# One load of a streaming decode kernel split by rows into sixteen loads of 1 to 15 rows

## The chip, the core and the metric

The kernel runs on one core of one Trainium2 chip. Times are device microseconds of one execution. The time before is 704.22 us, the median of three runs (703.95 to 704.27). The profile comes from one further execution, which took 704.12 us.

## The reference

A decode step of four sequences passes twice through the same pair of layers: grouped-query attention over a cache of 4096 positions, then a gated feed-forward block. Both passes use the same weights and the same caches, all in f32.

```python
B, Sq, D = 4, 1, 512
Hq, Hkv, Sk, Dh = 32, 8, 4096, 128          # F = 1792
q = (x @ wq).reshape(B, Sq, Hq, Dh)         # each K/V head serves 4 query heads
scores = einsum("bhqd,bhkd->bhqk", q, k) * Dh ** -0.5
o = einsum("bhqk,bhkd->bhqd", softmax(scores), v)
A = o.reshape(B, Sq, Hq * Dh) @ wo
h = silu(x @ w1) * (x @ w3);  B_ = h @ w2
x = x + A(layernorm(x)); x = x + B_(layernorm(x))     # and both once more
```

## The kernel before

**The data.** The host lays weights and caches side by side in one array `in_rows` of 128 rows. One unit of it is `KB` = 256 floats, so 1 KB of each row, 128 KB in all. Weights, and then the K and V tiles of each K/V head `g`, stand in the order of `stream`; a K or V tile is 4 units wide, `("kv", g, r)` with `r` from 0 to 31, the first 16 of K and the rest of V.

**The loads.** All data pass through one on-chip buffer, `space`, of 218 units (`SPACE`). The table `LOADS` lists every load by hand, in order: `(source unit, number of units, place in space)`. The function `pump` walks through the table and issues a load (L140; the first is on L137) as soon as its whole place is free; a place is set free by `done`, which the program calls after the last matmul that reads a tile. All loads are issued by SP, in the table's order, and go to one DMA queue. So a load that has to wait on SP holds up every later one.

**Completion counters.** The framework gives each load the next of eight completion counters in turn (`DMAHW0_49` to `DMAHW7_49` in the rows below). Before a load may take its counter, SP waits until the load eight places earlier, which had the same counter, has landed. Waits on `PE_49` mean that the place still has to be read by matmuls.

**The work.** Layer 0 goes through the heads 0 to 7, layer 1 from 7 back to 0, so that part of what is on the chip serves twice. For each head, `score` multiplies the query by the K tiles (L322), `maximum` and `exponent` make the softmax of half a head, `turn` transposes it and `weigh` multiplies it by the V tiles (L387). The weights follow: `project_o`, `gather_o`, `share_q`, and `feed_forward` with `down` (L503).

**The place of the change.** In layer 1, head 3, the entries `(544, 36, 148)` and `(580, 28, 190)` bring the V tiles `r` = 16 to 24 and 25 to 31. The last tile, `("kv", 3, 31)`, has its source at unit 604 and its place at 214. After it stand `(320, 64, 28)` and `(8, 24, 92)`, loads for the next heads, and `(384, 64, 154)`, whose place covers that of the last tile.

Of the kernel before, what the change touches and what calls it, by code (L numbers as in the profile page):

```python
# [16 lines left out]
P = 128  # L17
# [25 lines left out]
KB = 256  # L43
# [16 lines left out]
    (868, 8, 68), (876, 4, 186), (880, 4, 190), (884, 8, 194), ("stash", 1, 202), (892, 8, 206), ("stash", 0, 214),  # L60
# [5 lines left out]
)  # L66
BUSY = (4, 1, 2)
SCRATCH = 64

# [5 lines left out]
def tile_decode_layers(ctx: ExitStack, tc: tile.TileContext, rows, out):  # L75
    nc = tc.nc
# [9 lines left out]
    def place(at, n):  # L86
        return space[:, at * KB:(at + n) * KB]
# [32 lines left out]
    def pump():  # L120
        while state["next"] < len(LOADS):
            src, n, at = LOADS[state["next"]]
            if src == "stash":
                i, n = n, U // KB
                keys = [("kv", TURN, i)]
                if i == 0 and not state["back"]:
                    return
            else:
                keys = [key for key in stream if src <= offset[key] < src + n]
            if any(taken[at:at + n]):  # L130
                return
            taken[at:at + n] = [True] * n
            if src == "stash":
                for j in range(2):
                    nc.scalar.activation(place(at, n)[:, j * BLOCK:(j + 1) * BLOCK], stored[2 * i + j], AF.Copy)
            elif state["next"] == 0:
                nc.sync.dma_start(space[:, at * KB:], rows[:, 0:n * KB + P])  # L137
            else:
                lo = src * KB + (P if src >= LOADS[0][1] else 0)
                nc.sync.dma_start(place(at, n), rows[:, lo:lo + n * KB])  # L140
            for key in keys:
                where[key] = at
                at += size[key[0]]
            state["next"] += 1
# [4 lines left out]
    def done(layer, *key):  # L149
        if layer == 0 and (key[0][:2] == "w1" or key[0] in ("wq", "wo") and key[1] >= HELD or key[:2] == ("kv", TURN) and key[2] in KEPT):  # L150
            return
        at, n = where[key], size[key[0]]
        taken[at:at + n] = [False] * n
        pump()

    pump()


# [40 lines left out]
    def busy(n):  # L199
        if n:  # L200
            pt = scores().rearrange("p (k c) -> p k c", k=KC)
            nc.tensor.matmul(pt[:, 0:n, :], ident, ident.unsqueeze(1).to_broadcast([P, n, P]),  # L202
                             start=True, stop=True)
# [31 lines left out]
    def layernorm():  # L235
        xc, sq = deviation()
        xT = lay_down(xc)
        squares(xc, sq)

        def factor():  # L240
            var = o_ps[1][:, 1:2]
            mean(var, ssq)
            inverse(rstd[:, 0:1], var)

        return xT, factor
# [173 lines left out]
    def turn_o(o, oT):  # L419
        nc.tensor.matmul(misc[:, 0:B * REP], o, head, start=True, stop=True)  # L420
        nc.vector.tensor_copy(oT[:, :, 0:B], misc[:, 0:B * REP].rearrange("p (b h) -> p h b", b=B))  # L421
# [5 lines left out]
    def project_o(layer, g, oT):  # L427
        w = wo_of(g)
        for h in range(REP):
            for k in range(KC):  # L430
                nc.tensor.matmul(x_ps[32 * k:32 * k + B, :], oT[:, h, 0:B], w[:, h, k * P:(k + 1) * P],  # L431
                                 start=(h == 0), stop=(h == REP - 1))
        done(layer, "wo", g)
        nc.vector.scalar_tensor_tensor(x_sb, x_ps, 1.0, x_sb, op0=ALU.mult, op1=ALU.add,
                                       accum_out=rowsum)
# [107 lines left out]
    for layer in range(LAYERS):  # L543
# [13 lines left out]
        for n, (g, (first, last)) in enumerate(order):  # L557
# [7 lines left out]
            if layer and n == 0:  # L565
                state["back"] = True
                pump()
# [22 lines left out]
        nc.scalar.activation(spare, half[:, 0:1], AF.Sigmoid)  # L590
        busy(BUSY[0])
        turn_o(o, oT)
        busy(BUSY[1])
        project_o(layer, g, oT)
        busy(BUSY[2])
        xT, factor = layernorm()
# [50 lines left out]
```

## Time and profile before

| | |
|---|---|
| median of three runs | 704.22 us (703.95 to 704.27) |
| the profiled execution | 704.12 us, span 702.3 us |
| PE busy | 421.3 us (60%), 3280 matmuls |
| VectorE, ScalarE busy | 144.5 us (21%), 41.7 us (6%) |
| SP's DMA queue | 12960 packets, 297.41 MB, 99.0% of sixteen engines' time |
| rate over the span | 424 GB/s |
| mean granted TensorE clock | 0.825 |

The span is the time between the first and the last instruction of the profile; 1.8 us of the execution lie around it. PE is the matrix engine, SP the engine that issues the loads. "DMA share" in a table of stretches is the mean busy share of the core's sixteen DMA engines. "SPq" marks an instruction of SP's sequencer; in the timeline such rows are merged, "x4" with the time from the first start to the last end. In rows on DMA issues, the last number is the time from issue to landing, for the loads issued in the stretch that was asked for. Sizes are of all 128 rows together.

### The profile page before, as it was taken

How to read it: one execution, taken by the hardware profiler on the slowest of the kernel's cores; microseconds unless marked ns; L12 is line 12 of the kernel's file. 1: busy time of each engine (PE TensorE's matmuls, PEld its weight loads, DVE VectorE, ACT ScalarE, POOL GpSimd, SP SyncE). 2: the span in 40 equal slices, each digit the busy share in tenths (PEclk: the TensorE clock that was granted, in tenths of full speed). 3: DMA queues.
4: the chain of work that ended last, by engine and by line, in shares of the span. 5: the costliest groups of instructions: out<-in, count | busy, mean ns of one | idle time of the engine just before them, and what ended most of it. 6: DMA issues, size and time to landing. Idle time of an engine off the chain costs nothing.

```text
span 702.3 us, 7502 instructions
## 1 busy us (share of the span) xinstructions
PE 421.3 (60%) x3280; PEld 133.4 (19%) x3280; DVE 144.5 (21%) x512; ACT 41.7 (6%) x100; POOL 3.1 (0%) x10
## 2 busy tenths in 40 slices
PE   1265466644578409667688985744555734567576
PEld 0111121201112103121124221201111211121223
DVE  2012112121023103330231322112120301213221
ACT  0010000100001001000101210000100001000100
POOL 0000000000000000000000000000000000000000
PEclk9997677876769859886999997877877958779999
DMA  9999999999999999999999999999999999999996
GB/s 422 418 415 425 467 419 418 426 457 417 449 414 444 424 438 415 436 423 427 422 418 378 423 430 440 439 438 418 441 440 414 450 419 448 430 425 417 424 425 268
DMA packets 12991, 297.87 MB, mean 424 GB/s; under 512 B 1440, under 2 KB 1568, under 8 KB 4512
## 3 DMA queue, kind: packets, MB, share of 16 engines
q1 hardware_dynamic: 12960, 297.41, 99.0%
q8 instruction: 25, 0.41, 0.2%
q14 instruction: 6, 0.05, 0.0%
HBM read 297.34 MB, written 0.07 MB: 423 GB/s over the span
## 4 chain that ended last, share of the span: by engine, by line
DMA 71%; PE 24%; DVE 1%; another core or an unknown queue 1%; ACT 1%; issue 1%; SPq 0%; ACTq 0%; DVEq 0%
DMA space<-in_rows 71%; PE o L387 10%; PE scores L322 9%; PE sums_ps L306 1%; PE turned L348 1%; ACT p L341 1%; PE scores L202 1%; PE stored L251 1%; DVE acc L335 0%; DVE pT L350 0%; PE o L463 0%; SPq L140 0%; PE sums_ps L431 0%; PE sums_ps L420 0%
## 5 line engine op out<-in xcount | busy, mean ns | idle before, releaser
L322 PE MATMUL scores<-space,qT 128*32 128x512 f32 x1024 | 170.0, 713 | 141.6 <-DMA space<-in_rows 140.8
L387 PE MATMUL o<-space,pT 128*16 128x512 f32 x1024 | 152.8, 710 | 99.3 <-DMA space<-in_rows 91.5
L322 PEld LDWEIGHTS scores<-space,qT 128*32 128x32 f32 x1024 | 36.0, 123 | 218.6 <-issue 180.0
L387 PEld LDWEIGHTS o<-space,pT 128*16 128x16 f32 x1024 | 31.7, 108 | 198.3 <-issue 94.2
L335 DVE TENSOR_REDUCE acc<-scores 128x1 f32<-128x512 f32 x32 | 22.1, 691 | 181.5 <-PE scores L322 181.5
L341 ACT ACTIVATE p<-scores,acc 128x512 f32<-128x512 f32 x30 | 20.6, 687 | 559.0 <-DVE acc L335 432.1
L410 DVE SCALAR_TENSOR_TENSOR o<-o,acc,o 128x128 f32<-128x128 f32 x112 | 39.3, 351 | 49.2 <-PE o L387 45.8
L350 DVE COPY pT<-turned 128x256 f32<-128x256 f32 x32 | 13.6, 425 | 154.3 <-PE turned L348 154.3
L348 PE MATMUL turned<-ident,p 128*128 128x128 f32 x128 | 21.9, 296 | 11.8 <-ACT p L341 11.8
L295 PE MATMUL sums_ps<-space,xT 128*32 128x512 f32 x120 | 22.9, 704 | 2.4 <-DMA space<-in_rows 2.4
L421 DVE COPY o<-sums_ps 128x16 f32<-128x16 f32 x16 | 2.8, 175 | 98.1 <-PE sums_ps L420 98.1
L348 PEld LDWEIGHTS turned<-ident,p 128*128 128x128 f32 x128 | 14.0, 145 | 44.1 <-ACT p L341 25.7
L306 PEld LDWEIGHTS sums_ps<-same,shares 128*128 128x128 f32 x120 | 16.3, 211 | 16.8 <-DVE shares L301 11.1
L306 PE MATMUL sums_ps<-same,shares 128*128 128x4 f32 x120 | 17.6, 270 | 0.9 <-DVE shares L301 0.9
L463 PE MATMUL o<-space,xT 128*32 128x192 f32 (+1 forms) x256 | 13.7, 355 | 3.2 <-DMA space<-in_rows 1.5
L441 PE MATMUL stored<-space,o 128*32 128x512 f32 x104 | 13.5, 592 | 0.0
L301 DVE TENSOR_SCALAR shares<-sums_ps,columns 128x512 f32<-128x512 f32 x15 | 11.1, 743 | 1.7 <-PE sums_ps L295 1.7
L503 PE MATMUL sums_ps<-space,hT 128*4 128x128 f32 x224 | 9.1, 272 | 3.6 <-DMA space<-in_rows 2.9
L211 PE MATMUL o<-columns,same 128*32 128x1 f32 x64 | 2.0, 181 | 14.3 <-DVE columns L548 13.3
L420 PEld LDWEIGHTS sums_ps<-columns,o 128*128 128x128 f32 x32 | 6.1, 239 | 20.6 <-issue 13.0
L463 PEld LDWEIGHTS o<-space,xT 128*32 128x32 f32 x256 | 7.6, 110 | 8.4 <-DVE h L480 2.8
L420 PE MATMUL sums_ps<-columns,o 128*128 128x16 f32 x32 | 7.7, 318 | 0.6 <-DVE o L410 0.6
(101 smaller groups left out, 141.9 us busy)
## 6 DMA issues: line engine op xcount, KB each, us to landing
space<-in_rows SPq DMA_DIRECT2D x11, 4096.0 KB, 21.6
space<-in_rows SPq DMA_DIRECT2D x14, 1024.0 KB, 18.6
space<-in_rows SPq DMA_DIRECT2D x3, 4608.0 KB, 24.6
space<-in_rows SPq DMA_DIRECT2D x2, 6144.0 KB, 30.9
space<-in_rows SPq DMA_DIRECT2D x6, 2048.0 KB, 29.2
space<-in_rows SPq DMA_DIRECT2D x3, 3584.0 KB, 23.5
space<-in_rows SPq DMA_DIRECT2D x2, 5120.0 KB, 28.7
space<-in_rows SPq DMA_DIRECT2D x1, 7680.0 KB, 33.8
```

The lines of the kernel that those rows point to most:

```text
L295: nc.tensor.matmul(wide[32 * k:32 * k + 32, :], xT[:, 32 * k:32 * k + 32], w[:, k, :], start=True, stop=True)
L306: nc.tensor.matmul(misc[:, h * B:(h + 1) * B], shares[:, h * DH:(h + 1) * DH], same[:, 0:B], start=True, stop=True)
L322: nc.tensor.matmul(ps[32 * b:32 * b + 32, :], qT[:, b, at:at + 32], t[:, i * BLOCK:(i + 1) * BLOCK], start=(m < 2), stop=(m >= TILES - 2))
L335: nc.vector.tensor_reduce(acc[:, i:i + 1], ps, axis=AX.X, op=ALU.max, negate=True)
L341: nc.scalar.activation(p.rearrange("p n s -> p (n s)"), ps, AF.Exp, bias=acc[:, i:i + 1], scale=1.0 if scale is None else scale, accum_out ...
L348: nc.tensor.transpose(pt[:, n, :], p[:, n, :], ident)
L350: nc.vector.tensor_copy(pT, pt.rearrange("p n (b r) -> p n b r", b=B)[:, :, :, 0:ROW])
L387: nc.tensor.matmul(o_ps[i][32 * b:32 * b + ROW, :], pT[:, r // 2, b, :], t[:, j * NB * DH:(j + 1) * NB * DH], start=(r < 2), stop=(r >= TI ...
L410: nc.vector.scalar_tensor_tensor(o, o_ps[s][:, j * DH:(j + 1) * DH], acc[:, 16 + NB * s + j:17 + NB * s + j], o, op0=ALU.mult, op1=ALU.add)
L420: nc.tensor.matmul(misc[:, 0:B * REP], o, head, start=True, stop=True)
L441: nc.tensor.matmul(bank[32 * h:32 * h + 32, :], oT[:, h, :], w[:, h, :], start=first, stop=last)
L463: nc.tensor.matmul(bank[32 * j:32 * j + 32, s], xT[:, 32 * k:32 * k + 32], w[:, j], start=(k == 0), stop=(k == KC - 1))
```

## The change

The entry `(580, 28, 190)` is cut in two: `(580, 24, 190)` and `(604, 4, 214)`. The second, 4 KB of each of the 128 rows, is issued as sixteen DMAs: of 1 row, of 2, 3 and so on to 15, and of the 8 rows that remain. Sources and places in `space` stay as they were, and every other load too.

```diff
-    (580, 28, 190), (320, 64, 28), (8, 24, 92), (384, 64, 154), (192, 64, 28), (256, 64, 140), (32, 32, 28),
+    (580, 24, 190), (604, 4, 214), (320, 64, 28), (8, 24, 92), (384, 64, 154), (192, 64, 28), (256, 64, 140), (32, 32, 28),
...
+BY_ROWS = 604
+ROWS = 0, 1, 3, 6, 10, 15, 21, 28, 36, 45, 55, 66, 78, 91, 105, 120, P
...
-                nc.sync.dma_start(place(at, n), rows[:, lo:lo + n * KB])
+                for a, b in zip(ROWS, ROWS[1:]) if src == BY_ROWS else ((0, P),):
+                    nc.sync.dma_start(place(at, n)[a:b], rows[a:b, lo:lo + n * KB])
```

On SP, before, around the place of the change; the sizes are rows x floats of each row, so 128x9216 is the entry `(544, 36, 148)`, 128x7168 the entry `(580, 28, 190)`, and 128x16384 and 128x6144 behind it are `(320, 64, 28)` and `(8, 24, 92)`:

```order
L140 DMA space<-in_rows 128x9216 [waits DMAHW3_49,DMAHW1_49,PE_49]
L140 DMA space<-in_rows 128x7168 [waits PE_49]
L140 DMA space<-in_rows 128x16384 [waits DMAHW2_49,PE_49]
L140 DMA space<-in_rows 128x6144 [waits PE_49]
L140 DMA space<-in_rows 128x16384 [waits DMAHW4_49,DMAHW3_49,PE_49]
```

On SP in the changed kernel, the first rows of the same place; 128x6144 is now `(580, 24, 190)`:

```order
L143 DMA space<-in_rows 128x9216 [waits DMAHW3_49,DMAHW1_49,PE_49]
L143 DMA space<-in_rows 128x6144 [waits PE_49]
L143 DMA space<-in_rows 1x1024 [waits PE_49]
L143 DMA space<-in_rows 2x1024
L143 DMA space<-in_rows 3x1024
L143 DMA space<-in_rows 4x1024 [waits DMAHW0_49]
L143 DMA space<-in_rows 5x1024
L143 DMA space<-in_rows 6x1024 [waits DMAHW2_49]
```

The rows that follow them:

```order
L143 DMA space<-in_rows 7x1024 [waits DMAHW3_49]
L143 DMA space<-in_rows 8x1024 [waits DMAHW4_49]
L143 DMA space<-in_rows 9x1024 [waits DMAHW5_49]
L143 DMA space<-in_rows 10x1024 [waits DMAHW6_49]
L143 DMA space<-in_rows 11x1024 [waits DMAHW7_49]
L143 DMA space<-in_rows 12x1024 [waits DMAHW0_49]
L143 DMA space<-in_rows 13x1024 [waits DMAHW1_49]
L143 DMA space<-in_rows 14x1024 [waits DMAHW2_49]
L143 DMA space<-in_rows 15x1024 [waits DMAHW3_49]
L143 DMA space<-in_rows 8x1024 [waits DMAHW4_49]
L143 DMA space<-in_rows 128x16384 [waits DMAHW5_49,PE_49]
L143 DMA space<-in_rows 128x6144 [waits DMAHW6_49,PE_49]
```

Sixteen issues stand between the load of 3072 KB and that of 8192 KB. The load of 3072 KB has counter 4, the sixteen have the counters 5, 6, 7, 0 and so on round twice, and the load of 8192 KB has counter 5 again. The seventh small load waits on counter 3 for the load of 9216 floats a row; the eighth waits on counter 4 for the 3072 KB load; the ninth to the sixteenth wait for the first to the eighth; the load of 8192 KB waits on counter 5 for the ninth.

On PE, in `weigh` of head 3, the last rows that read the split tile, before and now:

```order
L387 MATMUL o_95<-space,pT 16x512 [waits DVE_49]
L387 MATMUL o_95<-space,pT 16x512
L387 MATMUL o_95<-space,pT 16x512 [waits DMAHW4_49]
L387 MATMUL o_95<-space,pT 16x512 x13
L322 MATMUL scores<-space,qT 32x512 [waits DMAHW5_49,PE_49]
```

```order
L390 MATMUL o_95<-space,pT 16x512 [waits DVE_49]
L390 MATMUL o_95<-space,pT 16x512
L390 MATMUL o_95<-space,pT 16x512 [waits DMAHW4_49]
L390 MATMUL o_95<-space,pT 16x512 x11
L390 MATMUL o_95<-space,pT 16x512 [waits DMAHW4_49,DMAHW5_49,DMAHW3_49,DMAHW6_49,DMAHW2_49,DMAHW7_49,DMAHW1_49,DMAHW0_49]
L390 MATMUL o_95<-space,pT 16x512
L325 MATMUL scores<-space,qT 32x512 [waits DMAHW5_49,PE_49]
```

The last two matmuls of the half head now wait for all eight counters, that is for the sixteen small loads; before, all tiles from `r` = 25 on came with one wait.

## The prediction

> **What bounds the kernel now.** I read the page first: its head, the slices, the queue and the chain that ended last.
>
> ```profile
> span 702.3 us, 7502 instructions
> DMA  9999999999999999999999999999999999999996
> q1 hardware_dynamic: 12960, 297.41, 99.0%
> DMA 71%; PE 24%; DVE 1%; another core or an unknown queue 1%; ACT 1%; issue 1%; SPq 0%; ACTq 0%; DVEq 0%
> ```
>
> The sixteen DMA engines are busy in every slice but the last, SP's queue alone fills 99.0% of their time, and the chain is 71% DMA. So the kernel lasts as long as 297 MB take to stream in, and what counts is any moment at which a DMA engine has nothing queued. Next I asked for busy time and DMA share in stretches around the changed load, from there to the end, and at the end.
>
> ```profile
> core 0: us, PE busy (x) PEld busy (x) DVE busy (x) ACT busy (x) POOL busy (x), PEclk, DMA share, GB/s
> 545.00:550.00 5.00, 5.00 (x44) 1.97 (x42) 0.55 (x2) 0.00 (x0) 0.00 (x0) 1.00 1.00 430
> 558.00:694.00 136.00, 80.96 (x685) 26.95 (x685) 28.38 (x100) 7.68 (x18) 0.55 (x1) 0.81 1.00 427
> 694.00:695.00 1.00, 0.63 (x17) 0.32 (x16) 0.41 (x3) 0.00 (x0) 0.00 (x0) 1.00 0.92 348
> 695.00:696.00 1.00, 0.73 (x28) 0.72 (x32) 0.00 (x0) 0.00 (x0) 0.00 (x0) 1.00 0.62 234
> 696.00:697.00 1.00, 0.72 (x29) 0.39 (x20) 0.00 (x0) 0.00 (x0) 0.00 (x0) 1.00 0.48 184
> 697.00:698.00 1.00, 0.45 (x20) 0.22 (x13) 0.00 (x0) 0.00 (x0) 0.00 (x0) 1.00 0.23 86
> 698.00:699.00 1.00, 0.80 (x24) 0.24 (x12) 0.00 (x0) 0.00 (x0) 0.00 (x0) 1.00 0.06 23
> ```
>
> The share is 1.00 up to 694 us, so a stall of the queue around 550 us finds no idle time later that could take it up. At the end the share falls in steps: the engines run out one by one over some 4.5 us, so they are uneven, and the slowest sets the end. The idle shares of those five rows add up to 2.7 us; that is the most that perfectly even engines could save.
>
> **The place of the change.** SP's issues and the DMA issues of narrow windows give the load that is split (3584 KB), the one behind it (third row of the second fence, where its 8192 KB stand without a size), and the load of 4608 KB before it.
>
> ```profile
> 520.83 0.33 SPq L140 DMA_DIRECT2D space<-in_rows  x1
> 525.56 32.82 SPq L140 DMA_DIRECT2D space<-in_rows  x4
> 545.36 4.84 SPq L140 DMA_DIRECT2D space<-in_rows  x2
> ```
>
> ```profile
> space<-in_rows SPq DMA_DIRECT2D x1, 4608.0 KB, 24.6
> space<-in_rows SPq DMA_DIRECT2D x1, 3584.0 KB, 28.3
> space<-in_rows SPq DMA_DIRECT2D x1, 27.9
> ```
>
> The load of 3584 KB is issued at 525.56 and lands 28.3 later, at 553.9. The next, of 64 rows of KB, is issued at 545.36 and lands at 573.3: its 8192 KB take 573.3 - 553.9 = 19.4 us, or 422 KB per us, 26.4 for each engine. When it is issued, 8.5 us of queue are still ahead of it. That is the cover which the change must not use up.
>
> **The change part by part.** Removed: 512 KB of the one load, 512/422 = 1.2 us of streaming. Its first 3072 KB keep their place and now land at about 552.7. The same 512 KB come back as sixteen loads, so the bytes cost nothing by themselves.
>
> Added: the sixteen issues, and their waits. The order shows that each load takes the next of eight completion counters, and that SP waits before a load until the load eight places earlier has landed. The seventh small load waits for the load of 4608 KB, so until 520.83 + 24.6 = 545.4; the eighth waits for the 3072 KB load itself, so until 552.7. Behind it on SP stand eight more small loads and then the load of 8192 KB, which before went out at 545.36. So the queue runs dry: at 552.7 the engines have only the 28 rows of seven small loads left. That is the term that decides, and it has two unknowns: the price of an issue, and that of starting the engines again.
>
> Issue:
>
> ```profile
> L140 SPq DMA_DIRECT2D space<-in_rows x88: 327/328/1182, 1.2 to 686.2; - x88
> 652.17 1.75 SPq L140 DMA_DIRECT2D space<-in_rows  x4
> ```
>
> Four issues in a row take 1.75 us, 0.44 each; the instruction alone has a median of 0.328 us. No issue of fewer than 128 rows is in the trace. The lower bound is 0.33; the upper is 0.44 with one slow one (1.18) among the nine. I take 0.44. The wait ends at 552.7 plus some 0.05, the eighth to sixteenth small loads are nine issues, and the big load is the tenth: 552.75 + 9 x 0.44 = 556.7. The small loads' own waits do not hold this up: the sixteenth waits for the eighth, issued 3.5 us before.
>
> Starting again:
>
> ```profile
> 0.74 0.38 SPq L137 DMA_DIRECT2D space<-in_rows  x1
> space<-in_rows SPq DMA_DIRECT2D x1, 4160.0 KB, 12.2
> out<-space SPq DMA_DIRECT2D x1, 64.0 KB, 1.5
> ```
>
> The program's first load meets idle engines: 4160 KB in 12.2 us, of which 4160/422 = 9.9 are streaming, so 2.3 us lie between issue and landing beyond the stream. The store at the end also meets idle engines: 1.5 - 64/422 = 1.35 us. The bounds are 1.35 and 2.3; I take 2.3, since that row is a load of the same kind on all sixteen engines. The Trainium skill, page "DMA: Bandwidth & Descriptors", section "Anatomy of one DMA", puts the fixed part of a DMA at about 2.0 us (measured on another issuing path); by that figure the sum below would be 0.3 us less, and the trace's 2.3 agrees roughly.
>
> Sum: the big load's stream now ends 2.3 + 19.4 us after 556.7, at 578.4; before it landed at 573.3. That is 5.1 us later, and each load behind it is as much later, since the share of 1.00 leaves no room. The 1.2 us of bytes are in the sum already: they land while SP issues.
>
> Priced at nothing: PE's matmuls on the split tile. They are the last of these:
>
> ```profile
> 554.37 3.67 PE o L387 x32
> 558.06 41.85 DMA space<-in_rows
> ```
>
> The sixteenth small load is issued at 552.75 + 8 x 0.44 = 556.3 and lands at 557.8 to 558.6, while PE now finishes the tile at 558.04. So PE, and with it the load that SP issues at 558.06 when that space is free, may be up to 1 us later. That load has 11,264 KB queued ahead of it (8192, and the 3072 of the second issue in the row of 545.36), 26.7 us, which hide it.
>
> The 16 engines start afresh together after the gap. The lead that the faster ones had at 550 us is lost, and that costs nothing, since the slowest sets each landing.
>
> Base and result: the profiled execution took 704.12 us with a span of 702.3 and 1.8 around it; the median of the runs is 704.22, 0.1 more. 704.12 + 5.1 = **709.2 us**.
>
> **The rivals.**
>
> *The queue does not run dry.* If SP could send the sixteen loads well before 550 us, only the uneven shares would act. If a load of n rows uses n engines with one row each, the first engine gets sixteen rows of 4 KB instead of eight and the last none: 8 x 4/26.4 = 1.2 us more and 1.2 us less. With the late engine of the end rows among those relieved, the time would be 704.12 - 1.2 = 702.9; with it among the loaded ones, 705.3. It decides if the eighth small load goes out more than a microsecond or two before the 3072 KB have landed. Against it stands the wait in the order; for it, that the engines are uneven indeed. The Trainium skill, same page, section "Why a DMA increments its semaphore by 16 and not by 1", says that a DMA on this queue takes the largest number of engines up to 16 that divides its slowest dimension, and the lowest-numbered ones; no row here shows it.
>
> *The stall is made up later.* Then the time stays at 704.1. It needs 5 us of idle DMA after 558 us; the row of 558 to 694 has 1.00, which speaks against it.
>
> *The small loads land late.* If the eighth takes not 1.5 but the shortest time that a load shows here, 5.1 us, the sixteenth waits for it until 552.75 + 5.1 = 557.85, and the big load goes out at 558.3: 6.7 us, 710.8. The row:
>
> ```profile
> DMA to landing us min/median/max: 5.1/21.0/51.5
> ```
>
> Against it: those loads had others queued ahead, these do not.
>
> *Each small load pays its way alone.* If the eighth to sixteenth followed each other at 1.5 us, issue to landing, the big load would go out at 552.75 + 9 x 1.5 = 566.3, 9.6 us later than forecast: 718.8. Against it: four issues stand within 1.75 us, long before any of them lands, and the counters make a load wait for the eighth before it only. The Trainium skill, same page, section "Rules for kernel authors", says that transfers under 64 KB pay mostly overhead and are to be joined into larger ones; that speaks against this change, and as far as the stall of 5.1 us goes I expect the trace to agree.
>
> **How the numbers follow.** Chances: the stall as summed 0.80; late landing 0.08; one by one 0.03; no dry queue 0.05 (0.03 faster, 0.02 slower); made up later 0.04. About 0.2%, 1.4 us, is what a measurement of this kernel can tell from no change. So slower 0.93, same 0.04, faster 0.03. The range takes in both unknowns: low ends, 9 x 0.33 and 1.35, give 552.75 + 3.0 + 1.35 - 553.9 = 3.2, or 707.3; the high ends, 0.44 with one issue of 1.18 (4.7 us) and 2.3, give 5.9, or 710.0. I stretch it to the late landing, 710.9. One by one, no dry queue and made up later, 0.12 together, stay outside.
>
> **What the new profile would show.** DMA share well under 1.00 between about 552 and 558 us, where it is 1.00 now; the sixteen issues, of which the last nine come in one run after 552.7 and about 0.44 apart; the 8192 KB load issued near 556.7 instead of 545.36; later pieces of the chain late by about 5 us. I am wrong if the 8192 KB load still goes out before 552 us, if the share stays at 1.00, or if the late pieces win back what the gap cost. If the gap is there with another length, the price of an issue or of the restart is the step that failed.

## The result, and the profile after

The changed kernel takes 709.18 us (median, 708.84 to 710.56) against 704.25 in runs beside it: ratio 1.0069, 95% interval 1.0055 to 1.0082, so slower. The prediction was 709.2. The profiled execution took 709.12 us with a span of 707.3, 5.0 more than before on both counts.

The page of the changed kernel, its head, queue and chain:

```profile
span 707.3 us, 7525 instructions
DMA  9999999999999999999999999999999899999997
q1 hardware_dynamic: 13216, 297.41, 98.5%
DMA 73%; PE 23%; DVE 1%; another core or an unknown queue 1%; SPq 1%; issue 1%; ACT 0%; DVEq 0%; ACTq 0%
```

The same 297.41 MB now fill 98.5% of the engines' time instead of 99.0%, the slice that holds the place of the change (548 to 566 us) has an 8, and SP's sequencer is now 1% of the chain instead of 0%. SP's timeline gives the run of small loads and the 8192 KB load behind them; the chain shows the same place step by step.

```profile
526.29 1.94 SPq L143 DMA_DIRECT2D space<-in_rows  x6
534.39 11.18 SPq L143 DMA_DIRECT2D space<-in_rows  x2
552.74 3.31 SPq L143 DMA_DIRECT2D space<-in_rows  x9
556.15 0.36 SPq L143 DMA_DIRECT2D space<-in_rows  x1
```

```profile
526.29 26.43 DMA space<-in_rows
552.72 0.02 issue
552.74 0.27 SPq L143
553.01 0.04 issue
553.05 0.29 SPq L143
...
555.32 0.38 SPq L143
555.71 0.04 issue
555.75 1.93 DMA space<-in_rows
```

The 3072 KB load and five small ones go out from 526.29 on; the sixth waits until 534.39, the seventh until 545.3, the eighth until the 3072 KB have landed at 552.72. Then nine small loads are issued in a row, and the load of 8192 KB goes out at 556.15, 10.8 us later than before. The stretches show what the DMA engines did meanwhile:

```profile
core 0: us, PE busy (x) PEld busy (x) DVE busy (x) ACT busy (x) POOL busy (x), PEclk, DMA share, GB/s
545.00:550.00 5.00, 5.00 (x46) 2.09 (x48) 0.92 (x4) 0.17 (x1) 0.00 (x0) 1.00 0.98 419
551.00:553.00 2.00, 2.00 (x16) 0.61 (x8) 0.00 (x0) 0.00 (x0) 0.00 (x0) 1.00 0.13 49
553.00:555.00 2.00, 1.48 (x17) 0.48 (x20) 1.73 (x11) 0.00 (x0) 0.00 (x0) 1.00 0.29 78
555.00:557.00 2.00, 2.00 (x19) 0.32 (x8) 1.32 (x5) 0.00 (x0) 0.00 (x0) 1.00 0.53 127
558.00:694.00 136.00, 76.82 (x620) 24.54 (x624) 26.68 (x96) 7.41 (x18) 0.55 (x1) 0.80 0.99 424
```

For six microseconds the queue moves 49 to 127 GB/s instead of over 400. Afterwards it is full again. (These views count a packet whole in the stretch in which it starts, so shares and rates of short stretches are rough, and a share can pass 1.00. With each packet of the trace spread over its own time, the three stretches from 551 to 557 us have shares of 0.25, 0.27 and 0.54.)

### The profile page after: what moved, and what is told of

It reads as the page before. It is cut to its first block, busy times and chain, and to the rows that moved or that the text cites. A ratio compares the mean times of both kernels' runs of the same rounds, so it can differ in the third digit from the quotient of the medians.

```text
span 707.3 us, 7525 instructions
## 1 busy us (share of the span) xinstructions
PE 420.5 (59%) x3280; PEld 135.5 (19%) x3280; DVE 144.4 (20%) x512; ACT 41.7 (6%) x100; POOL 3.0 (0%) x10
## 3 DMA queue, kind: packets, MB, share of 16 engines
q1 hardware_dynamic: 13216, 297.41, 98.5%
## 4 chain that ended last, share of the span: by engine, by line
DMA 73%; PE 23%; DVE 1%; another core or an unknown queue 1%; SPq 1%; issue 1%; ACT 0%; DVEq 0%; ACTq 0%
DMA space<-in_rows 73%; PE o L390 10%; PE scores L325 7%; PE turned L351 1%; PE sums_ps L309 1%; SPq L143 1%; PE stored L254 1%; PE sums_ps L298 0%; DVE pT L353 0%; DVE o L413 0%; PE o L466 0%; PE sums_ps L434 0%; PE scores L205 0%; ACT p L344 0%
## 5 line engine op out<-in xcount | busy, mean ns | idle before, releaser
L325 PE MATMUL scores<-space,qT 128*32 128x512 f32 x1024 | 173.3, 724 | 154.6 <-DMA space<-in_rows 153.9
L390 PE MATMUL o<-space,pT 128*16 128x512 f32 x1024 | 145.8, 675 | 90.1 <-DMA space<-in_rows 81.9
L351 PE MATMUL turned<-ident,p 128*128 128x128 f32 x128 | 23.5, 312 | 10.4 <-ACT p L344 10.4
L298 PE MATMUL sums_ps<-space,xT 128*32 128x512 f32 x120 | 24.4, 736 | 4.3 <-DMA space<-in_rows 4.3
L309 PEld LDWEIGHTS sums_ps<-same,shares 128*128 128x128 f32 x120 | 17.8, 227 | 17.4 <-DVE shares L304 10.2
L309 PE MATMUL sums_ps<-same,shares 128*128 128x4 f32 x120 | 19.1, 282 | 0.9 <-DVE shares L304 0.9
```

What stands on the lines that cost most here:

```text
L298: nc.tensor.matmul(wide[32 * k:32 * k + 32, :], xT[:, 32 * k:32 * k + 32], w[:, k, :], start=True, stop=True)
L309: nc.tensor.matmul(misc[:, h * B:(h + 1) * B], shares[:, h * DH:(h + 1) * DH], same[:, 0:B], start=True, stop=True)
L325: nc.tensor.matmul(ps[32 * b:32 * b + 32, :], qT[:, b, at:at + 32], t[:, i * BLOCK:(i + 1) * BLOCK], start=(m < 2), stop=(m >= TILES - 2))
L351: nc.tensor.transpose(pt[:, n, :], p[:, n, :], ident)
L390: nc.tensor.matmul(o_ps[i][32 * b:32 * b + ROW, :], pT[:, r // 2, b, :], t[:, j * NB * DH:(j + 1) * NB * DH], start=(r < 2), stop=(r >= TI ...
```

## The experiments

Two theories stood against each other first. *Dry queue*: the eighth small load waits for the load before the sixteen, so the queue runs empty; the price depends on how many loads follow it. *The small loads themselves*: each costs a fixed amount, or they burden the engines unevenly. The runs change the number and the form of the small loads; where a run also cuts the load before them, this is said.

### Six loads, seven, sixteen and thirty-two with even shares

```diff
-ROWS = 0, 1, 3, 6, 10, 15, 21, 28, 36, 45, 55, 66, 78, 91, 105, 120, P
+ROWS = 0, 16, 32, 48, 64, 96, 128
...
+ROWS = 0, 16, 32, 48, 64, 80, 96, 128
...
+ROWS = 0, 16, 32, 48, 64, 80, 96, 112, 128
+PARTS = 2
...
+                    w = n * KB // PARTS if src == BY_ROWS else n * KB
+                    for c in range(0, n * KB, w):
+                        nc.sync.dma_start(place(at, n)[a:b, c:c + w], rows[a:b, lo + c:lo + c + w])
```

The first line is that of six loads, the second that of seven; the rest is that of sixteen, and thirty-two differ from it by `PARTS = 4`.

> The same 512 KB as six loads (four of 16 rows, two of 32), all on sixteen engines. Theory (the queue runs dry, because a small load that stands eight places behind the 3072 KB load has to wait for its landing): the 8192 KB load now stands seven places behind, so it waits only for the load of 4608 KB and goes out near 545.4 as before; DMA share stays 1.00 around 550 us; 704.2 us. Rival 'each small load costs a fixed amount' (5.0 us / 16 = 0.31 each): 704.2 + 6 x 0.31 = 706.1. Rival 'uneven shares of the engines': shares are even here, 704.2.

> The same 512 KB as seven loads (six of 16 rows, one of 32). Theory (dry queue): now the 8192 KB load itself stands eight places behind the 3072 KB load, so it goes out at 552.8 instead of 545.4; no issue stands between, but the engines have at most the small loads, 1.2 us, to cover a restart of 2.3 to 2.7 us; 704.2 + 1.1 to 1.5 = 705.3 to 705.7. Rival 'fixed amount each': 704.2 + 7 x 0.31 = 706.4, only 0.3 above the six loads. Rival 'uneven shares': 704.2.

> The same 512 KB as sixteen loads of 16 rows x 2 KB each, so all on sixteen engines, 32 KB each. Theory (dry queue): as in the changed kernel, nine issues and a restart after the landing at 552.7; issues of 16 rows are taken at 0.43 instead of the 0.38 measured there: 5.0 + 9 x 0.05 = 5.4 later, 709.6. Rival 'fixed amount each': 709.2. Rival 'uneven shares': shares are even, 704.2.

> The same 512 KB as thirty-two loads of 16 rows x 1 KB. Theory (dry queue): twenty-five issues of 0.43 and a restart after 552.7: the 8192 KB load goes out at 552.75 + 25 x 0.43 = 563.5, 7.4 later than in the changed kernel, so 709.2 + 7.4 = 716.6. Rival 'fixed amount each': 704.2 + 32 x 0.31 = 714.2. Rival 'uneven shares': 704.2.

Measured, beside 703.97 of the kernel before: six 706.7 (ratio 1.0037, 1.0025 to 1.0049), seven 706.79 (1.0049, 1.0037 to 1.0062), sixteen 710.2 (1.0088, 1.0075 to 1.0101), thirty-two 717.58 (1.0193, 1.018 to 1.0206). Even shares do not save anything, so the uneven shares are not the cause. Sixteen and thirty-two follow the dry queue (709.6 and 716.6) within 1.0 us; sixteen would fit the fixed price as well (709.2), thirty-two would not (714.2). But six was expected at 704.2 and took 2.7 more, and fits the fixed price (706.1) better. Seven, expected at 705.3 to 705.7, took 1.1 more than that, and only 0.1 more than six: in this form the step from six to seven does not show in the time. The stretches of six:

```profile
545.00:550.00 5.00, 5.00 (x50) 2.20 (x52) 1.11 (x5) 0.40 (x1) 0.00 (x0) 1.00 1.01 415
550.00:553.00 3.00, 2.79 (x24) 0.76 (x14) 0.53 (x3) 0.68 (x3) 0.00 (x0) 1.00 1.29 314
553.00:557.00 4.00, 3.21 (x26) 0.72 (x30) 2.90 (x14) 0.00 (x0) 0.00 (x0) 1.00 1.06 342
```

There is no gap: the DMA share is over 1.00 while the rate is only 314 and 342 GB/s. The engines were busy but slow. (With each packet spread over its own time, the shares are 1.03 and 1.01, the rates 255 and 284 GB/s.) In the trace's packet records the 4 KB packets took 0.273 us (median), and the last packets of the 3072 KB load, which ran beside them, 1.58 us where 0.91 is usual. So a second cost exists, and the next runs take it apart.

### Six loads in two other forms, and seven

The same 512 KB as six loads of all 128 rows with 512 or 768 B of each; as six loads of 32 rows that lie four rows apart; and as seven loads of all rows.

```diff
+PIECES = [(slice(0, P), slice(a, b)) for a, b in ((0, 128), (128, 256), (256, 448), (448, 640), (640, 832), (832, 1024))]
...
+PIECES = [(slice(r, P, 4), slice(a, b)) for r, a, b in ((0, 0, 1024), (1, 0, 1024), (2, 0, 512), (2, 512, 1024), (3, 0, 512), (3, 512, 1024))]
...
+                for rs, cs in PIECES if src == BY_ROWS else ((slice(0, P), slice(0, n * KB)),):
+                    nc.sync.dma_start(place(at, n)[rs, cs], rows[:, lo:lo + n * KB][rs, cs])
```

> After the six loads of 16 to 32 neighbouring rows, which cost 2.7 us with no gap in the queue: their packets of 4 KB took about 0.28 us beside each other, 1.8 times the 0.156 of a lone one, so the new theory is that many engines writing to few neighbouring rows get in each other's way. Here the 512 KB go as six loads of all 128 rows, 512 or 768 B of each. Theory (dry queue from the seventh load on, and neighbouring rows slow): neither applies, 704.2 us, the 8192 KB load issued near 545.4. Rival 'each extra small load costs by itself' (2.7 / 6 = 0.45 each): 706.7.

> Six loads again, of 32 rows each, four rows apart (4 KB of each row in two of them, 2 KB in four). Theory (neighbouring rows get in each other's way): the same number of rows in a load as in the larger of the six loads before, but spread over all 128, so no loss: 704.2. Rival 'few rows or small loads are slow wherever they lie': 706.7, as with neighbouring rows.

> Seven loads of all 128 rows, 512 or 768 B of each. Theory (dry queue): one load more than six puts the 8192 KB load eight places behind the 3072 KB load; it goes out at 552.8 instead of 545.4, and the restart is only partly covered: 705.3 to 705.7, that is 1.1 to 1.5 above the six loads of all rows. Rival 'each extra small load costs by itself': 704.2 + 7 x 0.45 = 707.4 if the six loads of all rows take 706.7, and no step between six and seven.

Measured, beside 704.01: all rows 704.38 (ratio 0.9999, 0.9985 to 1.0014), four rows apart 704.09 (0.9995, 0.9979 to 1.001), seven 705.53 (1.0013, 0.9999 to 1.0027). Six loads more cost nothing if they cover all rows or their rows are spread, so a fixed price for each load falls. Rates of the six loads of all rows, then of those four rows apart (384 and 426, then 420 and 432 GB/s, with each packet spread over its own time):

```profile
550.00:553.00 3.00, 3.00 (x28) 0.65 (x20) 1.23 (x6) 1.08 (x3) 0.00 (x0) 1.00 1.28 476
553.00:557.00 4.00, 3.48 (x34) 1.25 (x36) 2.92 (x14) 0.00 (x0) 0.00 (x0) 1.00 1.05 450
```

```profile
550.00:553.00 3.00, 3.00 (x27) 0.89 (x20) 0.81 (x6) 1.07 (x3) 0.00 (x0) 1.00 1.20 498
553.00:557.00 4.00, 3.48 (x35) 0.92 (x33) 3.06 (x14) 0.00 (x0) 0.00 (x0) 1.00 1.12 484
```

And the step from six to seven loads is there in SP's timeline, six first: the first issue of each row is the 8192 KB load.

```profile
545.25 0.33 SPq L143 DMA_DIRECT2D space<-in_rows  x1
```

```profile
552.71 0.81 SPq L143 DMA_DIRECT2D space<-in_rows  x2
```

One small load more moves it from 545.25 to 552.71, as the counters have it. The time rises by 1.15 us in the medians, in the expected range (705.3 to 705.7); by the ratio alone, seven loads are only just not distinguished from before.

### Sixteen spread loads in one go, and woven

Sixteen loads of 32 rows x 1 KB, four rows apart: once in one go, once in fours between three pieces of 1024 KB; and the changed kernel's own sixteen loads woven in the same way.

```diff
+LAST = [(slice(r, P, 4), slice(24 * KB + c, 25 * KB + c)) for r in range(4) for c in range(0, 4 * KB, KB)]
+PIECES = [q for i in range(4) for q in (*LAST[4 * i:4 * i + 4],
+          *[(slice(0, P), slice(8 * i * KB, 8 * i * KB + 8 * KB))][:i < 3])]
```

> Sixteen loads of 32 rows x 1 KB, the rows four apart (which cost nothing in the six strided loads), in one go as in the changed kernel. Theory (dry queue): issues of such loads stood 0.62 apart in the run of six, so nine of them take 5.6 us instead of 3.4: 709.2 + 2.2 = 711.4. Rival 'neighbouring rows make the loss of the changed kernel': no neighbours here, 704.2.

> The very same sixteen strided loads, but woven in fours between the 3072 KB, which go as three loads of 1024 KB: four small, one large, four small, one large, and so on. No load waits for one that stands last in the queue, and something is always left in it. Theory (dry queue): 704.2 to 705.5, with the 8192 KB load issued before the last of the large pieces has landed. Rival 'sixteen more loads cost what they cost wherever they stand': 711.4, as in one go.

> The changed kernel's own sixteen loads of 1 to 15 neighbouring rows, woven in the same way. Theory: without the dry queue only the price of neighbouring rows is left, which was 2.7 us for six loads of 16 and 32 rows: 705 to 707.5. Rival 'the sixteen row loads cost 5.0 us wherever they stand': 709.2.

Measured, beside 704.23: in one go 711.35 (ratio 1.0101, 1.0087 to 1.0115), woven 706.58 (1.0033, 1.0022 to 1.0045), own rows woven 706.65 (1.0044, 1.003 to 1.0058). SP's run of nine small loads and the 8192 KB load, in one go, and its stretch:

```profile
552.84 6.19 SPq L143 DMA_DIRECT2D space<-in_rows  x10
```

```profile
553.00:557.00 4.00, 3.48 (x29) 0.81 (x28) 3.06 (x14) 0.00 (x0) 0.00 (x0) 1.00 0.17 41
```

Without neighbouring rows the sum of the dry queue comes out at once: 711.4 expected, 711.35 measured. The very same loads, woven, are 4.8 us faster. That they are not at 704.2 to 705.5, as expected, is mostly because the weave was too loose: the share is 0.76 from 545 to 550 us, so the queue ran partly dry there. At the 430 GB/s of the kernel before, the bytes of that stretch would have taken 2.1 us less, of the 2.4 that this run lost. The 8192 KB load went out at 552.88, 2 us before the last of the large pieces landed (554.84), as expected, but long after 545.4.

```profile
545.00:550.00 5.00, 5.00 (x44) 1.97 (x42) 0.55 (x1) 0.00 (x0) 0.00 (x0) 1.00 0.76 252
```

The changed kernel's own loads, woven, cost 2.4 us instead of 4.9. How much of these 2.4 is the loose weave and how much neighbouring rows was not separated.

### Uneven shares without a dry queue: two attempts

```diff
+PIECES = [(slice(32, P), slice(0, 12 * KB)), *((slice(r, 32, 4), slice(0, 12 * KB)) for r in range(4))]
...
+ROWS = 0, 127, 128
```

> Uneven shares without a dry queue: the load of 28 rows of KB is cut into 16 and 12, and the 12 KB part goes as one load of 96 rows and four of 8 rows that lie four rows apart. If a load of 8 rows uses the first eight engines only, they get ten rows of 12 KB each and the others six instead of eight: 24 KB or 0.9 us more and less. The 8192 KB load stands six places behind the 2048 KB load, so no gap. If the late engines of the end are in the second half: 703.3; if they are in the first half: 705.1; if a load of 8 rows is spread over all sixteen: 704.2.

> Uneven shares alone: the 512 KB as two loads, of 127 rows and of 1 row, 4 KB each; only three places from the 3072 KB load to the 8192 KB load, so no dry queue. The Trainium skill, page 'DMA: Bandwidth & Descriptors', section 'Why a DMA increments its semaphore by 16 and not by 1', names 127 partitions as a case that uses one engine. By rows of this case: one engine then carries 127 packets of 0.156 us, 19.8 us instead of 1.2, and ends 18.6 us later less the lead it has over the slowest, 0 to 4.5 us: 718.3 to 722.8. If the 127 rows are spread over the engines, or the other engines take over, 704.2. The distance tells what an uneven share costs when no other cause hides it.

The first took 708.53 (ratio 1.0055, 1.0038 to 1.0072) where 703.3 to 705.1 was expected. It says nothing on shares: while its pieces ran, the rate fell with the engines busy, as with the six loads of neighbouring rows. The slow stretch begins with the load of 96 neighbouring rows, ahead of those of 8: in the packet records its 12 KB packets take 0.9 us from 548 us on, where 0.46 is usual, and the 16 KB packets of the load before them 1.2 instead of 0.61. So loads of few rows are not the only slow ones.

```profile
549.00:553.00 4.00, 4.00 (x34) 1.06 (x27) 1.48 (x6) 1.07 (x3) 0.00 (x0) 1.00 1.07 232
```

The second took 728.63 (1.0356, 1.0339 to 1.0373), 6 us over its range of 718.3 to 722.8. One engine did carry the 127 rows: the share between 550 and 555 us is 0.15, and the trace has 4 KB packets one behind the other from 549.5 to 578 us. Its 8192 KB load had landed on fifteen engines by 581.87 us and on the sixteenth at 598.73, 25.5 us later than before (573.26); the whole time is 24.7 us longer. The expectation lacked two things. The 127 packets took 28.8 us rather than 19.8: 0.16 each until 557.7 us, but 0.28 on average once 64 KB packets of the other engines ran beside them. And SP was held up, as its timeline has it:

```profile
525.33 30.68 SPq L143 DMA_DIRECT2D space<-in_rows  x2
```

```profile
550.00:555.00 5.00, 4.48 (x40) 1.28 (x36) 2.25 (x14) 1.08 (x3) 0.00 (x0) 1.00 0.15 61
```

The issue of the single row behind the 127 did not end until 556.0, so the 8192 KB load was late too, and the other engines stood idle. So this run shows that a large uneven share is paid by the one engine that has it, but the price of a small one stays open. That the changed kernel's loss is not that of uneven shares follows from the sixteen spread loads, and from its own packet records: the first sixteen packets of the 8192 KB load, read here as one for each engine, begin between 557.14 and 557.92 us, so by then no engine had a backlog left.

## Why the prediction was right

**The dry queue** was the step that decided, and it is shown three times: by the share of 0.13 to 0.53 after 551 us, by the jump of the 8192 KB load from 545.25 to 552.71 between six and seven loads, and by 4.8 us between the same sixteen loads in one go and woven.

**The landing at 552.7** came as summed, at 552.72.

**The price of an issue** was taken too high. The tenth issue, the big load, was to go out at 556.7; it went out at 556.15, nine issues in 3.4 us, 0.38 each instead of 0.44. The chain shows the durations: the instruction takes 0.27 us for 8 rows and 0.38 for 15, with 0.04 between two. Spread rows are dearer: 0.62 apart in the run of sixteen.

**The restart** was taken too low. PE starts on the 8192 KB load's data at 578.97, and before at 573.39:

```profile
578.97 3.54 PE L325 MATMUL scores<-space,qT 128*32 128x512 f32 x16 [19.79 <-DMA space<-in_rows]
```

```profile
573.39 3.64 PE L322 MATMUL scores<-space,qT 128*32 128x512 f32 x16 [15.40 <-DMA space<-in_rows]
```

From 556.15 to the landing just before 578.97 are 22.7 us, and 19.4 of stream leave 3.3 for the restart, not 2.3. The first packets of 64 KB, all sixteen started at once, took 3.2 us (median) where 2.42 is usual. In the run of sixteen spread loads the same span, from issue to landing, is 22.4 us, so neighbouring rows have little part in it. The load is thus 5.6 us late rather than 5.1: the two terms were off by -0.5 and +1.0.

**The lead of the faster engines** was priced at nothing, and that step was wrong. The prediction said that the engines start afresh together, that the lead of the faster ones is lost, and that this costs nothing. It pays: the engine that was behind is no longer behind. In the trace a load of all rows steps its counter sixteen times, read here as once for each engine. Before, the steps of the 8192 KB load are 3.0 us apart from first to last, now 1.3; for the last load from `in_rows` it is 4.5 and 2.2 us. The mean over the sixteen is 6.0 us later than before at both loads, so the stall itself is never made up; the last engine, which sets the time, is 5.6 us later at the one and 5.0 at the other. The five rows at the end, whose idle shares added up to 2.7 us before, now add up to 1.7:

```profile
699.00:700.00 1.00, 0.62 (x17) 0.32 (x16) 0.41 (x3) 0.00 (x0) 0.00 (x0) 1.00 1.00 403
700.00:701.00 1.00, 0.73 (x28) 0.72 (x32) 0.00 (x0) 0.00 (x0) 0.00 (x0) 1.00 1.03 397
701.00:702.00 1.00, 0.68 (x28) 0.39 (x20) 0.00 (x0) 0.00 (x0) 0.00 (x0) 1.00 0.79 291
702.00:703.00 1.00, 0.47 (x20) 0.20 (x12) 0.00 (x0) 0.00 (x0) 0.00 (x0) 1.00 0.40 143
703.00:704.00 1.00, 0.82 (x24) 0.26 (x15) 0.00 (x0) 0.00 (x0) 0.00 (x0) 1.00 0.08 31
```

The other runs bear this out: the three with six loads, which had no gap, end with 4.0 to 4.6 us between the first and the last engine; the eight in which the 8192 KB load went out only after 552 us, that of 127 rows aside, with 2.0 to 2.6. So 709.2 against 709.18 is in part luck: an issue price 0.5 us too high and a gain of 0.6 at the end that was not foreseen make up for a restart 1.0 too low.

**PE's matmuls on the split tile**, priced at nothing, end at 559.2 instead of 558.04, as forecast within 0.2 us. The load behind them is issued at 559.21 and lands 47.2 us later; 19.4 of these are its own 8192 KB, so it met 27.8 us of queue, which hid the delay.

**The rivals.** The queue did run dry. The stall was not made up, as the means over the engines show. The small loads did not land late: the sixteenth took 1.93 us. They did not pay their way one by one: nine went out in 3.3 us. The rule of the Trainium skill that the prediction cited (page "DMA: Bandwidth & Descriptors", section "Rules for kernel authors") says that transfers under 64 KB pay mostly overhead. The sixteen have 4 to 60 KB and cost 4.9 us; to that extent the runs agree. But sixteen spread loads of 32 KB cost 7.1 us in one go and 2.4 woven, so most of the price here lies in where they stand. The six spread loads, which were free, have 64 to 128 KB and so lie outside the rule.

What the prediction did not see is the cost of neighbouring rows. In the changed kernel it stayed hidden: its late 4 KB packets took 0.24 us (median) instead of 0.16, but while they ran, the engines were busy for about half their time at most (0.27 and 0.54 from 553 to 557 us), waiting for SP's issues.

## What to carry to other kernels

When one load becomes many, count the loads that may be in flight: from the first one that has to wait for the load ahead of the group, every further issue is paid in full, with a restart on top, less what the engines gain by starting together again (about 1 us at the end of this kernel). Six pieces fitted under the queue here, the seventh did not. Pieces that cover all rows, or rows spread evenly over all 128, cost nothing there; pieces of 16, 32 or 96 neighbouring rows slowed even the large load beside them.

## What the runs showed of the hardware

While loads of 16 and 32 neighbouring rows ran, the queue moved 314 to 342 GB/s with every engine busy; with the same bytes in 32 rows four apart, 484 to 498 by the same view. With each packet spread over its own time, these are 255 to 284 and 420 to 432 GB/s. The Trainium skill, page "SBUF — State Buffer", section "Door 1: The DMA port swizzle (why `[64,N]` ≈ `[32,N]`)", says that a transfer's rate depends on how many of 16 ports its rows reach, and that four neighbouring rows share one; that agrees with 0.273 us for a 4 KB packet of neighbouring rows and 0.159 for one of spread rows. Whether the loads of 16 rows, which the spread form does not have, play a part of their own was not separated, and no run tells the ports apart.

The load of 127 rows ran on one engine: its 4 KB packets come one behind the other from 549.5 to 578.3 us. The Trainium skill, page "DMA: Bandwidth & Descriptors", section "Why a DMA increments its semaphore by 16 and not by 1", says this of 127 rows; the trace agrees. Beyond it, the next load on SP, of one row, needed 30.3 us to issue, without a semaphore to wait for. It ended at 556.0, when the engine had begun 42 of the 127 packets. This looks as if the engine's backlog held up SP itself, and so the work of all the others; no run tests it.
